# Quarter tiles of the TensorE array for the convolution and part of the products, unsplit chunk 2, blocks of 510 tokens

## Chip, cores, metric

The kernel runs on 1 core of a Trainium2 chip. The metric is the device time in microseconds (us), median of several executions. Engines: PE is TensorE (PEld its weight loads), DVE is VectorE, ACT is ScalarE, POOL is GpSimd, SP is SyncE, which here only issues DMAs.

## What is computed

`x` is 8 x 4224 tokens x 192 channels, float32. First a causal convolution of 7 taps, whose weights are a softmax for each of 8 heads (24 channels a head):

```python
w = exp(weight - max); w = w / (sum(w) + 1e-9)         # (8 heads, 7 taps)
y[b, s, h, :] = sum_k w[h, k] * xpad[b, s + k, h, :]   # causal
```

Then, with y as input:

```python
gate_pre = sum_k conv_w[k] * ypad[:, k:k+S, :]         # 5 taps for each channel, causal
gate = 1 / (1 + exp(-gate_pre))
out = (gate * (y @ w_val)) @ w_out                     # both matrices 192 x 192
```

## The kernel before

The host lays out the input; the kernel does all arithmetic. The batch is seen as 2 streams of 4 sequences each, end to end, 16936 tokens a stream with padding. A stream is cut into **supers** of mostly 976 tokens (2 runs of 488, of which 972 are new), and a super into two **blocks** of mostly 486 tokens (`SPLIT`). The 192 channels are two **chunks**: chunk 1 has 16 channels of each head (128 channels, on 128 partitions, once for each stream: parts 0 and 1, tile `xa`), chunk 2 has 8 of each head (64 channels, both streams on 128 partitions: part 2, tile `xb`).

Convolution (`mm`, line 504). A matmul takes 128 consecutive positions of 64 channels as its stationary operand (from `xin`, which `xw` fills) and the head's band matrix (`band`, 128 x 122) as its moving operand, and gives 122 outputs on 64 partitions. Two such matmuls, for the two halves of the output partitions, use the array's column halves (shape 128*64). A super takes 48 of these float32 matmuls; the trace records each as two weight loads and two matmuls. ACT copies the banks to `e` (line 521), and DMAs issued by SP move the rows to the channel order of `xa` and `xb` (line 538).

Gate. For each part ACT multiplies by the first tap (line 592), DVE adds the four others (line 598), ACT takes the sigmoid (line 604).

Products. `product` makes V = y @ w_val and O = (gate * V) @ w_out in four pieces by chunk: `p11` (128 to 128 channels, line 643, for each stream), `p21` (chunk 2 into chunk 1, line 632, on the array's row halves, 64*128), `p22` (chunk 2 to chunk 2 with a block-diagonal matrix, line 648), `p12` (chunk 1 into chunk 2, line 619, column halves, plain float32). Pieces 11, 21 and 22 run in float32r: the operand is split into a high part (ACT cast, lines 575 and 700) and the rest (POOL subtraction, lines 579 and 704), and three passes are summed:

```python
            def passes(q):
                h, l = halfs(q)
                return (wh[kind], h), (wl[kind], h), (wh[kind], l)
```

V leaves PSUM in the multiplication with the gate: on DVE for parts 1 and 2 (line 689), and for part 0 through an ACT copy `va` (line 680) and POOL (line 683). O leaves by an ACT copy to `ot` (line 716), and SP issues one store for a block.

Order. `Scheduler` simulates the engines with a cost for each operation and writes out one order for each engine; priorities are a block's due time (`tau`, spaced by `BLOCK`) plus an offset of the kind of operation (`PR`). For PE it knows modes (C for column halves, R for row halves, F for the full array), and prefers to stay in a mode. The kernel follows that order, so each engine's queue is in order. PSUM: 6 banks (`pv`) for convolution and products, 2 (`pg`) for the gate taps.

At the start PE multiplies zeros (line 391), ACT and DVE make the band, and DVE decodes the weight matrices, which come as 64-bit floats (lines 403 to 424).

Of the kernel before, what the change touches and what calls it, by code (L numbers as in the profile page):

```python
# [20 lines left out]
HALO = KG - 1  # L21
WIN, WK = 122, 128
# [5 lines left out]
MB = 488  # L28
# [4 lines left out]
RUNS = [122, 244] + [488] * 16 + [332]  # L33
SPLIT = {122: [240], 244: [484], 488: [486, 486], 332: [484, 176]}
# [3 lines left out]
def cuts(n):  # L38
    return [(o, min(WIN, n - o)) for o in range(0, n, WIN)]


class Super:
    def __init__(self, g, start):
        self.g, self.start, self.run = g, start, RUNS[g]
        self.toks = 2 * self.run
        self.blocks = SPLIT[self.run]
        assert sum(self.blocks) == self.toks - HALO
        self.runs = (self.run, self.run // 2)
        self.cuts = tuple(cuts(r) for r in self.runs)
        self.items = []  # L50
        self.banks = []
# [4 lines left out]
        self.loads = []  # L56
        self.where = {}
        for c in (1, 0):
            w = 128 * len(self.cuts[c])
            for q in range(4):  # L60
                if not self.loads or self.loads[-1] + w > 1024:
                    self.loads.append(0)
                self.where[c, q] = len(self.loads) - 1, self.loads[-1]
                self.loads[-1] += w
# [15 lines left out]
FLAT = max(p.start + p.toks for p in SUPERS) + WK  # L80
AT = [3 * sum(s[2] for s in STEPS[:n]) for n in range(N + 1)]

# [19 lines left out]
class Scheduler:  # L102
    LAG = {"PE": 260, "ACT": 200, "DVE": 200, "POOL": 200, "DMA": 100}
    SAME = {"PE": 0, "ACT": 120, "DVE": 127, "POOL": 100}
    SWITCH, STICK, HASTE = 190, 10000, 2.0
    PATIENCE = {"PE": 0, "ACT": 0, "DVE": 0}
    RATE, FLIGHT, LAND = 320.0, 900, 600
# [35 lines left out]
    def run(self):  # L143
# [11 lines left out]
        mode, dma = None, 0.0  # L155
        events = [(0.0, -1, None)]
        done, order = 0, []
        n = 0
        while events:
# [11 lines left out]
            while again:  # L171
                again = False
                for e in engines:
# [30 lines left out]
                    ns = o.ns  # L204
# [4 lines left out]
                    o.eng, o.at = e, t  # L209
                    busy[e] = t + ns  # L210
                    if o.kb:
                        dma = max(dma, t + ns + self.FLIGHT) + o.kb * 1000.0 / self.RATE
                        o.end = dma + self.LAND
                    else:
                        o.end = t + ns
# [25 lines left out]
NR, NW = 384, 448  # L241
HALVES = (slice(0, 64), slice(64, 128))

POOLS = {"x": 6, "e": 9, "x1": 3, "x2": 3, "xs": 2, "g": 3, "ps": 2, "ot": 3, "va": 2, "pv": 6, "pg": 2}
FULL_OUT = ()
POOL_GATE = (0,)
BLOCK = 9400.0
PR = {
    "load": -35000, "conv": -19500, "cstep": 1000, "row": -6000, "hx": -1500, "lx": -16000,
# [7 lines left out]
def kernel(  # L257
# [15 lines left out]
    def sb(name, shape, dt=F32):  # L273
# [3 lines left out]
        "x": [sb(f"xin{i}", [WK, 1024]) for i in range(POOLS["x"])],  # L277
# [3 lines left out]
        "xs": [  # L281
            (sb(f"xh{i}", [128, 2, MB], F32R), sb(f"xl{i}", [128, 2, MB], F32R), sb(f"yh{i}", [128, MB], F32R), sb(f"yl{i}", [128, MB], F32R))
            for i in range(POOLS["xs"])
        ],
        "g": [(sb(f"ga{i}", [128, 2, MB]), sb(f"gb{i}", [128, MB])) for i in range(POOLS["g"])],
        "ps": [
            {q: (sb(f"ph{q}{i}", [128, MB], F32R), sb(f"pl{q}{i}", [128, MB], F32R)) for q in range(3) if q not in FULL_OUT}
            for i in range(POOLS["ps"])
        ],
        "ot": [sb(f"ot{i}", [128, 3 * MB]) for i in range(POOLS["ot"])],  # L290
# [11 lines left out]

    def cast_ns(n):
# [4 lines left out]
    band = sb("band", [WK, NH, WIN])  # L308
# [11 lines left out]
    raw_v = slots["x"][-1][:, : 2 * NV].bitcast(I32)  # L320
    raw_o = slots["ot"][1][:, : 2 * NO].bitcast(I32)
    tmp = [slots["ot"][0][:, i * NV : (i + 1) * NV].bitcast(I32) for i in range(3)]
    tmp.append(slots["ot"][1][:, 2 * NO : 2 * NO + NV].bitcast(I32))
# [10 lines left out]
    boot_x, boot_ot, boot_raw = sc.buf("x"), sc.buf("ot"), sc.buf("ot")  # L334
    boot_x.slot, boot_ot.slot, boot_raw.slot = POOLS["x"] - 1, 0, 1
    sc.free["x"] = [(0, i) for i in range(POOLS["x"] - 1)]
    sc.free["ot"] = [(0, i) for i in range(2, POOLS["ot"])]
# [11 lines left out]
    for i in range(2):  # L349
        hs = slice(4 * i, 4 * i + 4)  # L350
        ld_bw.append(dma(f"bw{i}", "SP", lambda o, hs=hs: issue(o).dma_start(band[:, hs], bw[:, hs]), (), P0 + 1 + i, (), 250))
# [4 lines left out]
    t1 = sc.add("texp", "ACT", 1500, lambda o: nc.scalar.activation(warm[:, 0:1], one, AF.Exp), (z1,), P0)  # L356
# [13 lines left out]
    for i, h in enumerate((0, 4, 1, 5, 2, 6, 3, 7)):  # L370
        x = sc.add(
            f"exp{h}", "ACT", 240,
# [5 lines left out]
            f"band{h}", "DVE", 200,  # L378
# [52 lines left out]
    ld_wr = dma("wr", "SP", lambda o: issue(o).dma_start(raw_v, wr.bitcast(I32)), (), PW, (boot_x,), 404)  # L431
# [397 lines left out]
```

## Time and profile before

| | us |
|---|---|
| device time, median of 3 runs | 371.16 (369.92 to 372.65) |
| device time of the profiled execution | 370.18 |
| its span in the profile | 368.4 |
| busy in the span: PE / PEld / DVE / ACT / POOL | 356.9 / 285.2 / 340.6 / 342.6 / 289.1 |
| granted TensorE clock, mean | 0.998 |

The span runs from the first to the last instruction; 1.8 us of the device time lie outside it. Busy time is a union, so operations that overlap on their engine count once. Matmuls overlap too: the time that one costs is read from the start of one to the start of the next, not from its duration.

### The profile page before, as it was taken

Reading aid. Unit: us, or ns where it says so; the run is one execution under the profiler, and the core shown is the slowest. Engines: PE = TensorE matmul, PEld = TensorE weight load, DVE = VectorE, ACT = ScalarE, POOL = GpSimd, SP = SyncE. Lnnn points to the kernel's source line nnn. Section 1 sums busy time; section 2 is a strip of 40 time slices with the busy share of each in tenths; the row PEclk is TensorE's granted clock in tenths of the full one; section 3 lists DMA queues with packets and bytes.
Section 4 is the critical chain, followed back from the end, with each engine's and each line's share of the span. In section 5 each row is a group of like instructions: output and inputs, shape, how many; then the busy total and the mean of one; then the engine's idle time right before and its main releaser. Section 6 shows DMA issues by size and latency. Waiting matters only on the chain.

```text
span 368.4 us, 9449 instructions
## 1 busy us (share of the span) xinstructions
PE 356.9 (97%) x3362; PEld 285.2 (77%) x3362; DVE 340.6 (92%) x550; ACT 342.6 (93%) x662; POOL 289.1 (78%) x236
## 2 busy tenths in 40 slices
PE   8588999999999999999999999999999999999996
PEld 4476787787977787878888787888887878887674
DVE  4999999989999999899999999899989898999993
ACT  6459999998999999999999999999999999999985
POOL 1946998976868895969787878879696969787994
PEclk9999999999999999999999999999999999999999
DMA  7798855739495466758593939395857767444324
GB/s 244 227 322 269 263 230 210 245 129 316 161 322 228 171 221 209 283 209 285 203 294 110 328 142 322 145 315 180 290 195 233 252 225 234 163 165 162 115 81 191
DMA packets 36222, 81.87 MB, mean 222 GB/s; under 512 B 6096, under 2 KB 24400, under 8 KB 36176
## 3 DMA queue, kind: packets, MB, share of 16 engines
q1 hardware_dynamic: 35712, 80.59, 63.7%
q0 software_dynamic: 464, 0.69, 0.6%
q8 instruction: 26, 0.43, 0.5%
q14 instruction: 20, 0.16, 0.1%
HBM read 29.11 MB, written 26.01 MB: 150 GB/s over the span
## 4 chain that ended last, share of the span: by engine, by line
PE 92%; DMA 4%; ACT 1%; SPq 1%; DVE 0%; issue 0%; POOL 0%; ACTq 0%; POOLq 0%
PE bank L643 27%; PE bank L504 21%; PE bank L619 16%; PE bank L632 14%; PE bank L648 13%; DMA xb<-e 4%; PE bank L391 2%; SPq L538 1%; ACT bank L592 0%; ACT yh L575 0%; DVE bank L598 0%; DVE wlO L460 0%; POOL zero L354 0%; ACT gb L604 0%; ACT va L680 0%
## 5 line engine op out<-in xcount | busy, mean ns | idle before, releaser
L598 DVE SCALAR_TENSOR_TENSOR bank<-xa,cwt,bank 128x486 f32<-128x486 f32 (+3 forms) x216 | 151.5, 708 | 11.5 <-ACT bank L592 7.5
L504 PE MATMUL bank<-band,xin 128*64 128x122 f32 (+2 forms) x1696 | 92.6, 267 | 5.1 <-DMA xin<-xw 5.1
L504 PEld LDWEIGHTS bank<-band,xin 128*64 128x64 f32 x1696 | 89.2, 137 | 9.4 <-ACT bank L592 2.5
L704 POOL TENSOR_TENSOR pl<-ga,ph 128x486 fp32r<-128x486 f32 (+3 forms) x72 | 85.8, 1205 | 8.0 <-ACT ph L700 6.4
L579 POOL TENSOR_TENSOR xl<-xa,xh 128x972 fp32r<-128x972 f32 (+3 forms) x36 | 73.8, 2051 | 20.5 <-ACT xh L575 20.5
L598 DVE SCALAR_TENSOR_TENSOR bank<-xb,cwt,bank 128x486 f32<-128x486 f32 (+3 forms) x108 | 76.2, 706 | 1.3 <-ACT bank L592 0.5
L716 ACT COPY ot<-bank 128x486 f32<-128x486 f32 (+3 forms) x108 | 58.2, 559 | 8.8 <-PE bank L648 3.9
L521 ACT COPY e<-bank 128x488 f32<-128x488 f32 (+2 forms) x107 | 55.9, 577 | 6.0 <-PE bank L504 6.0
L683 POOL TENSOR_TENSOR ga<-va,ga 128x486 f32<-128x486 f32 (+3 forms) x36 | 43.2, 1201 | 18.4 <-ACT va L680 17.9
L579 POOL TENSOR_TENSOR yl<-xb,yh 128x486 fp32r<-128x486 f32 (+3 forms) x36 | 40.7, 1131 | 18.3 <-ACT yh L575 18.3
L598 DVE SCALAR_TENSOR_TENSOR ga<-xa,cwt,bank 128x486 f32<-128x486 f32 (+3 forms) x72 | 50.4, 701 | 2.0
L592 ACT ACTIVATE bank<-xa,cwt 128x486 f32<-128x486 f32 (+3 forms) x72 | 48.5, 673 | 0.1
L704 POOL TENSOR_TENSOR pl<-gb,ph 128x486 fp32r<-128x486 f32 (+3 forms) x36 | 43.3, 1202 | 2.0 <-ACT ph L700 2.0
L604 ACT ACTIVATE ga<-ga 128x486 f32<-128x486 f32 (+3 forms) x72 | 44.4, 618 | 0.2
L700 ACT CAST ph<-ga 128x486 fp32r<-128x486 f32 (+3 forms) x72 | 42.4, 602 | 0.0
L619 PE MATMUL bank<-ga,wfO 128*64 128x242 f32 (+3 forms) x288 | 36.1, 370 | 0.0
L575 ACT CAST xh<-xa 128x972 fp32r<-128x972 f32 (+3 forms) x36 | 35.7, 991 | 0.5 <-DMA xa<-e 0.5
L619 PE MATMUL bank<-xa,wfV 128*64 128x242 f32 (+3 forms) x288 | 34.4, 362 | 0.7 <-DMA xa<-e 0.7
L643 PE MATMUL bank<-xh,whV 128*128 128x486 f32 (+3 forms) x72 | 28.7, 399 | 1.2 <-DVE gb L689 1.2
L643 PE MATMUL bank<-ph,whO 128*128 128x486 f32 (+3 forms) x72 | 29.5, 409 | 0.0
L619 PEld LDWEIGHTS bank<-ga,wfO 128*64 128x64 f32 x288 | 18.2, 136 | 11.7 <-issue 6.8
L643 PE MATMUL bank<-pl,whO 128*128 128x486 f32 (+3 forms) x72 | 27.2, 378 | 0.0
(87 smaller groups left out, 660.7 us busy)
## 6 DMA issues: line engine op xcount, KB each, us to landing
xin<-xw SPq DMA_DIRECT2D x51, 512.0 KB, 6.3
out<-ot SPq DMA_DIRECT2D x32, 729.0 KB, 4.5
xa<-e SPq DMA_DIRECT2D x64, 244.0 KB, 2.4
xb<-e SPq DMA_DIRECT2D x128, 61.0 KB, 2.1
out<-ot SPq DMA_DIRECT2D x2, 726.0 KB, 3.5
xin<-xw SPq DMA_DIRECT2D x2, 384.0 KB, 7.4
xa<-e SPq DMA_DIRECT2D x4, 166.0 KB, 2.2
band<-bw SPq DMA_DIRECT2D x2, 244.0 KB, 3.0
```

What stands on the lines that cost most here:

```text
L504: nc.tensor.matmul(at(pc)[P, j * run + a : j * run + a + n], lhsT=t[:, off + 128 * w + 64 * h : off + 128 * w + 64 * h + 64], rhs=band[:, ...
L521: nc.scalar.copy(at(eb)[:, :n], at(pc)[:, :n])
L579: nc.gpsimd.tensor_tensor(out=s[2 * c + 1], in0=views(n)[c], in1=s[2 * c].bitcast(F32), op=ALU.subtract)
L592: lambda o, n=n, i=i, pg=pg, m=m: nc.scalar.mul(at(pg)[:, :m], part(n, i, 0), cwt[:, i // 2, 0:1]),
L598: v.scalar_tensor_tensor(out=acc if k < KG - 1 else gate(i), in0=part(n, i, k), scalar=cwt[:, i // 2, k : k + 1], in1=acc, op0=ALU.mult, o ...
L604: sig[i] = sc.add(f"s{n}.{i}", "ACT", 0.823 * m + 110, lambda o, i=i, gate=gate: nc.scalar.activation(gate(i), gate(i), AF.Sigmoid), (d, t ...
L619: nc.tensor.matmul(a[P, c], lhsT=wf[kind][:, W12 : W12 + 64], rhs=full_x(q)[:, c], start=new and i == 0, stop=not new and i == 1,)
L632: nc.tensor.matmul(at(acc[q])[:, :m], lhsT=a[P, W21 : W21 + 128], rhs=b[P], start=new[q] and i == 0, stop=not new[q] and i == 2,)
L643: nc.tensor.matmul(at(acc[q])[:, :m], lhsT=a[:, W11 : W11 + 128], rhs=b, start=new and i == 0, stop=not new and i == 2)
L648: nc.tensor.matmul(at(acc[2])[:, :m], lhsT=a[:, W22 : W22 + 128], rhs=b, start=new and i == 0, stop=not new and i == 2)
L704: nc.gpsimd.tensor_tensor(out=l, in0=gate(q), in1=h.bitcast(F32), op=ALU.subtract)
L716: lambda o, q=q, ob=ob, po=po, m=m: nc.scalar.copy(at(ob)[:, q * m : (q + 1) * m], at(po[q])[:, :m]),
```

## The change

- Convolution: windows of 64 positions give up to 58 outputs. A matmul uses a quarter of the array (64 rows, 64 columns); four of them, two heads' groups on the two row halves by two output halves, go one after another to the four quarters, and the row halves write two PSUM banks. A super of 1024 tokens (1020 new) has 9 cuts of 57 and 5 of 52 tokens, each for two pairs of groups: 112 matmuls.
- Piece 21 of V and O: four quarter matmuls in plain float32 (`mm21`). Piece 22 of V: column halves in plain float32 (`mmcol`). Piece 22 of O: quarters in plain float32, for two blocks at once; O's chunk 2 for two blocks lies in two banks (`x`, `y`), one for each stream, and is stored for the pair.
- Chunk 2 is no longer split: its ACT casts and POOL subtractions go, for y and for the gated values.
- Part 2 is gated on POOL like part 0 (one more ACT copy, DVE only has part 1).
- Blocks have 510 tokens; the last super has two blocks of 450 (before 484 and 176). Loads of `xin` have up to 640 columns (before 1024), 6 a super (before 3). Buffers, priorities and the planner's constants change with it, and the planner's mode R becomes Q (quarters), to which the convolution belongs as well. At the start, row moves of the first two supers are issued by POOL with ACT or SP, and the loads of three supers come first.

```diff
-WIN, WK = 122, 128
+WIN, WK = 58, 64
-MB = 488
+MB = 512
-RUNS = [122, 244] + [488] * 16 + [332]
-SPLIT = {122: [240], 244: [484], 488: [486, 486], 332: [484, 176]}
+RUNS = [116, 256] + [512] * 15 + [452]
+SPLIT = {116: [228], 256: [508], 512: [510, 510], 452: [450, 450]}
+LOADW = 640
...
 def cuts(n):
-    return [(o, min(WIN, n - o)) for o in range(0, n, WIN)]
+    k = -(-n // WIN)
+    s = -(-n // k)
+    return [(o, min(s, n - o)) for o in range(0, n, s)]
...
+        self.sets = []
         for c in (1, 0):
-            per = MB // self.runs[c]
-            for a in range(0, 4, per):
-                self.banks.append((c, list(range(a, min(4, a + per)))))
...
+            per = max(1, MB // self.runs[c])
+            for a in range(0, 2, per):
+                self.sets.append((c, [2 * i for i in range(a, min(2, a + per))]))
...
-POOL_GATE = (0,)
+POOL_GATE = ((0, 2),)
...
-            def mm(o, c=c, qs=qs, pc=pc, run=run, cc=cc, src=src, xb=xb):
...
-                    i, off = src[j]
-                    t = at(xb[i])
                     for w, (a, n) in enumerate(cc):
+                        i, off = p.where[c, q, w]
+                        t = at(xb[i])
                         for h, P in enumerate(HALVES):
-                            nc.tensor.matmul(
-                                at(pc)[P, j * run + a : j * run + a + n],
-                                lhsT=t[:, off + 128 * w + 64 * h : off + 128 * w + 64 * h + 64],
-                                rhs=band[:, head(c, q, h), :n], start=True, stop=True,
-                            )
-
-            ns = sum(2 * (0.80 * n + 8.5) for _, n in cc) * len(qs)
+                            for r, K in enumerate(HALVES):
+                                nc.tensor.matmul(
+                                    at(pcs[r])[P, j * run + a : j * run + a + n],
+                                    lhsT=t[K, off + 64 * h : off + 64 * h + 64],
+                                    rhs=band[K, head(c, q + r, h), :n], start=True, stop=True,
+                                )
+            ns = sum(2 * max(0.80 * n + 10, CONV_MIN) for _, n in cc) * len(qs)
...
+    def mm21(kind, banks, rhs, m):
+        def emit(o):
+            new = [b.open(0, 1) for b in banks]
+            for h, P in enumerate(HALVES):
+                for b, K, x in zip(banks, HALVES, new):
+                    nc.tensor.matmul(
+                        at(b.buf)[P, :m], lhsT=wf[kind][K, W21 + 64 * h : W21 + 64 * h + 64], rhs=rhs()[K], start=x, stop=not x,
+                    )
+        return emit
...
+    def mmcol(kind, off, pieces, m):
+        def emit(o):
+            new = [b.open(h) for b, h, _, _ in pieces]
+            for (b, h, w, rhs), x in zip(pieces, new):
+                nc.tensor.matmul(at(b.buf)[HALVES[h], :m], lhsT=wf[kind][:, off + w : off + w + 64], rhs=rhs(), start=x, stop=not x)
+        return emit
...
+            w = m * len(V_SPLIT)
+            h = sc.add(f"hx{n}", "ACT", cast_ns(w), hx, L[0], t0 + PR["hx"], None, (xb[0], xsb))
+            hs = [h, sc.add(f"lx{n}", "POOL", 2.0 * w + 265, lx, [h] + L[0], t0 + PR["lx"], None, (xb[0], xsb))]
...
+        o21 = sc.add(f"V21.{n}", "PE", fp32(m), mm21("V", (a, b), lambda: part(2), m), L[1] + fv, t0 + PR["V21"], "Q", (a.buf, b.buf, xb[2]))
...
+            sc.add(f"V12.{n}", "PE", fp32(m), mmcol("V", W12, [(c, h, 0, lambda h=h: part(h)) for h in range(2)], m), L[0] + fv, t0 + PR["V12"], "C", (c.buf, xb[0])),
+            sc.add(f"V22.{n}", "PE", fp32(m), mmcol("V", W22, [(c, h, 64 * h, lambda: part(2)) for h in range(2)], m), L[1] + fv + [zw[0]], t0 + PR["V22"], "C", (c.buf, xb[2])),
...
-            if q in POOL_GATE:
+            pb = pv[q].buf
+            if q in POOL_GATE[n % len(POOL_GATE)]:
...
+            if q in O_SPLIT:
+                sb_ = psb[q] = sc.buf("ps")
+                h = sc.add(f"hg{n}.{q}", "ACT", cast_ns(m), lambda o, q=q, sb_=sb_: nc.scalar.copy(at(sb_)[0][:, :m], gate(q)), (d,), t0 + PR["cast"], None, (gb[q], sb_))
...
+            x, y = Bank(), Bank()
+            def mm22(o):
+                new = [b.open(0, 1) for b in (x, y)]
+                for h, P in enumerate(HALVES):
+                    for b, K, w in zip((x, y), HALVES, new):
+                        nc.tensor.matmul(
+                            at(b.buf)[P, :m], lhsT=wf["O"][K, W22 + K.start : W22 + K.start + 64], rhs=gates[h](2)[K], start=w, stop=not w,
+                        )
+            o22 = sc.add(f"O22.{pair[0]}", "PE", fp32(m), mm22, [d[2] for d in dfs] + fo, t0 + PR["O22"], "Q", [x.buf, y.buf] + [b[2] for b in gbs])
+            pieces = [(b, h, 0, lambda h=h, q=q: gates[h](q)) for q, b in enumerate((x, y)) for h in range(2)]
+            o12 = sc.add(
+                f"O12.{pair[0]}", "PE", 2 * fp32(m), mmcol("O", W12, pieces, m), [d[q] for d in dfs for q in range(2)] + fo,
+                t0 + PR["O12"], "C", [x.buf, y.buf] + [b[q] for b in gbs for q in range(2)],
             )
...
+            send([(x, [o12, o22]), (y, [o12, o22])], k, tau[pair[1]], f"{pair[0]}p")
```

## Rows read from the trace of the kernel before

**Rows 1.** The page's first part: busy us of each engine, share of the span.

```profile
PE 356.9 (97%) x3362; PEld 285.2 (77%) x3362; DVE 340.6 (92%) x550; ACT 342.6 (93%) x662; POOL 289.1 (78%) x236
```

**Rows 2.** The page's fourth part: the chain that ended last, by engine and line.

```profile
PE 92%; DMA 4%; ACT 1%; SPq 1%; DVE 0%; issue 0%; POOL 0%; ACTq 0%; POOLq 0%
PE bank L643 27%; PE bank L504 21%; PE bank L619 16%; PE bank L632 14%; PE bank L648 13%; DMA xb<-e 4%; PE bank L391 2%; SPq L538 1%; ACT bank L592 0%; ACT yh L575 0%; DVE bank L598 0%; DVE wlO L460 0%; POOL zero L354 0%; ACT gb L604 0%; ACT va L680 0%
```

**Rows 3.** Windows: length; busy PE, PEld, DVE, ACT, POOL; clock, DMA share, GB/s.

```profile
7.60:30.00 22.40, 15.68 (x243) 13.66 (x242) 20.64 (x45) 12.31 (x27) 12.98 (x17) 1.00 0.79 263
...
132.67:152.36 19.69, 19.69 (x194) 16.00 (x193) 19.22 (x30) 19.22 (x38) 14.74 (x13) 1.00 0.70 237
152.36:172.04 19.68, 19.68 (x190) 16.14 (x188) 18.48 (x29) 19.07 (x37) 16.02 (x13) 1.00 0.69 236
...
350.00:368.40 18.40, 15.21 (x108) 11.16 (x106) 12.07 (x26) 12.91 (x32) 13.00 (x14) 0.96 0.35 136
```

**Rows 4.** Timeline of PE over one super, 152.36 to 172.04: start, us, operation.

```profile
152.36 5.17 PE L504 MATMUL bank<-band,xin 128*64 128x122 f32 x96
157.36 0.99 PE L619 MATMUL bank<-ga,wfO 128*64 128x242 f32 x8
158.18 0.99 PE L619 MATMUL bank<-xa,wfV 128*64 128x242 f32 x8
159.10 0.49 PE L643 MATMUL bank<-ph,whO 128*128 128x486 f32 x1
159.44 0.38 PE L643 MATMUL bank<-ph,wlO 128*128 128x486 f32 x1
159.66 0.39 PE L643 MATMUL bank<-pl,whO 128*128 128x486 f32 x1
...
166.46 0.45 PE L632 MATMUL bank<-pl,whO 64*128 64x486 f32 x2
166.84 0.49 PE L643 MATMUL bank<-xh,whV 128*128 128x486 f32 x1
167.17 0.38 PE L643 MATMUL bank<-xh,wlV 128*128 128x486 f32 x1
```

**Rows 5.** Timeline of PE around 8.1 us: convolution matmuls of 61 columns.

```profile
7.90 0.46 PE L504 MATMUL bank<-band,xin 128*64 128x61 f32 x10
```

**Rows 6.** Timeline of the weight loads in the same stretch.

```profile
7.91 0.38 PEld L504 LDWEIGHTS bank<-band,xin 128*64 128x64 f32 x10
```

**Rows 7.** Timeline of the weight loads around 144.6 us, row halves.

```profile
144.58 0.19 PEld L632 LDWEIGHTS bank<-pl,whO 64*128 64x128 f32 x2
```

**Rows 8.** Groups by shape, whole span: count, busy us, mean ns of one.

```profile
L504 PE MATMUL bank<-band,xin 128*64 128x61 f32 x16 | 0.7, 226 | 0.0
...
L598 DVE SCALAR_TENSOR_TENSOR bank<-xa,cwt,bank 128x240 f32<-128x240 f32 x6 | 2.8, 460 | 0.0
...
L521 ACT COPY e<-bank 128x332 f32<-128x332 f32 x6 | 2.3, 455 | 0.0
```

**Rows 9.** Groups by shape of ACT, window 152.36 to 172.04.

```profile
L521 ACT COPY e<-bank 128x488 f32<-128x488 f32 x6 | 3.1, 588 | 0.0
...
L575 ACT CAST yh<-xb 128x486 fp32r<-128x486 f32 x2 | 1.3, 632 | 0.0
...
L700 ACT CAST ph<-gb 128x486 fp32r<-128x486 f32 x2 | 1.2, 595 | 0.0
L680 ACT COPY va<-bank 128x486 f32<-128x486 f32 x2 | 1.2, 588 | 0.0
```

**Rows 10.** Groups by shape of DVE, same window.

```profile
L598 DVE SCALAR_TENSOR_TENSOR bank<-xa,cwt,bank 128x486 f32<-128x486 f32 x12 | 8.6, 726 | 1.0 <-ACT bank L592 0.7
...
L689 DVE TENSOR_TENSOR gb<-bank,gb 128x486 f32<-128x486 f32 x2 | 1.3, 665 | 0.1
```

**Rows 11.** Groups by shape of POOL, same window.

```profile
L579 POOL TENSOR_TENSOR yl<-xb,yh 128x486 fp32r<-128x486 f32 x3 | 3.5, 1171 | 1.0 <-ACT yh L575 1.0
...
L683 POOL TENSOR_TENSOR ga<-va,ga 128x486 f32<-128x486 f32 x2 | 2.5, 1233 | 1.2 <-ACT va L680 1.2
```

More of the change, by code (lines that the diff above doesn't have):

```diff
@@ L79 @@
 TM = max(p.toks for p in SUPERS)
-FLAT = max(p.start + p.toks for p in SUPERS) + WK
+FLAT = max(p.start + p.toks for p in SUPERS) + 2 * WK
 AT = [3 * sum(s[2] for s in STEPS[:n]) for n in range(N + 1)]
+PAIRS = []
+for _n in range(N):
+    if PAIRS and len(PAIRS[-1]) == 1 and STEPS[_n][0] == STEPS[_n - 1][0] and STEPS[_n][2] == STEPS[_n - 1][2]:
+        PAIRS[-1] += (_n,)
+    else:
+        PAIRS.append((_n,))
 def head(c, q, half):
@@ L276 @@
     slots = {
[L277 removed]
+        "x": [sb(f"xin{i}", [128, LOADW]) for i in range(POOLS["x"])],
         "e": [sb(f"e{i}", [128, MB]) for i in range(POOLS["e"])],
@@ L301, in small, with either, leave @@
         return 0.72 * n + 105
+    def either(n):
+        return {"ACT": 0.72 * n + 105, "DVE": 1.042 * n + 70}
+    def leave(o, dst, src):
+        if o.eng == "ACT":
+            nc.scalar.copy(dst, src)
+        else:
+            v.tensor_copy(dst, src)
     def cast_ns(n):
         return 0.823 * n + 100
-    band = sb("band", [WK, NH, WIN])
+    band = sb("band", [128, NH, WIN])
     hwt = sb("hwt", [128, NH, KW])
@@ L552, in part, with fp32, thrice, __init__ @@
         return x1[:, i] if i < 2 else x2
-    for n, (g, off, m) in enumerate(STEPS):
+    def fp32(m):
+        return 2 * (0.83 * m + 10)
+    def thrice(m):
+        return 3 * (0.431 * m + 9.5)
+    class Bank:
+        def __init__(self):
+            self.buf, self.fresh, self.made = sc.buf("pv"), [True, True], []
+        def open(self, *halves):
+            new = any(self.fresh[h] for h in halves)
+            for h in halves:
+                self.fresh[h] = False
+            return new
@@ new lines, in mm21, with mm11 @@
+    def mm21(kind, banks, rhs, m):
[7 more added lines that the diff above has]
+        return emit
+    def mm11(kind, bank, rhs, split, m, mode):
+        def emit(o):
+            new = bank.open(0, 1)
+            d = at(bank.buf)[:, :m]
+            if split is not None:
+                h, l = split()
+                for i, (a, b) in enumerate(((wh[kind], h), (wl[kind], h), (wh[kind], l))):
+                    nc.tensor.matmul(d, lhsT=a, rhs=b, start=new and i == 0, stop=not new and i == 2)
+            elif mode == "F":
+                nc.tensor.matmul(d, lhsT=wf[kind][:, W11 : W11 + 128], rhs=rhs(), start=new, stop=not new)
+            else:
+                for h, P in enumerate(HALVES):
+                    nc.tensor.matmul(d[P], lhsT=wf[kind][:, W11 + 64 * h : W11 + 64 * h + 64], rhs=rhs(), start=new, stop=not new)
+        return emit
@@ L702, in lg @@
-            def lg(o, q=q, gsplit=gsplit, gate=gate):
-                h, l = gsplit(q)
-                nc.gpsimd.tensor_tensor(out=l, in0=gate(q), in1=h.bitcast(F32), op=ALU.subtract)
-            l = sc.add(f"lg{n}.{q}", "POOL", 2.0 * m + 265, lg, (h, d), t0 + PR["rest"], None, (gb, psb))
-            dh[q], dl[q] = [h], [l]
-        keep = {0: [gb, psb], 1: [gb, psb], 2: [psb, gb]}
-        ro = product("O", po, lambda q, gsplit=gsplit: gsplit(q), lambda q, gate=gate: gate(q), dh, dl, df, tuple(t0 + PR["O" + k] for k in "FRC"), f32=FULL_OUT, keep=keep)
@@ L730 @@
+    for pair in PAIRS:
+        for n in pair:
+            gate_and_value(n)
+        output(pair)
     order = sc.run()
@@ L784, in packed @@
         return p.reshape(128, -1)
-    bw = np.full((WK, NH, WIN), FILL, f)
+    bw = np.full((128, NH, WIN), FILL, f)
     for k in range(KW):
         j = np.arange(WIN)
-        bw[j + k, :, j] = weight[:, k]
+        for r in (0, WK):
+            bw[r + j + k, :, j] = weight[:, k]
     arrays = {
```

437 lines of the change are left out of this document (226 added, 211 removed), and 7 rows, old and new, of the table PR.

## Prediction

> **What bounds the kernel now.** I read the busy times first [rows 1]: PE 97%, ACT 93%, DVE 92%. Shares so close don't name a limit, so I went to the chain that ended last [rows 2]: 92% of it is PE, with five matmul lines as its parts and 4% of DMA. The windows show where [rows 3]: from the middle on, a super (972 new tokens) takes 19.69 us, and PE is busy in all of it (19.68 of 19.68), at the full granted clock, with ACT at 19.07 and DVE at 18.48. The two other engines have 0.6 and 1.2 us of air in a super. So what the change is worth is PE time in a super, until ACT takes over. 16936 tokens at 19.69 us for 972 make 343.1 us; the other 25.3 us of the 368.4 are the start and the end (in the stretch from 7.6 to 30 us PE is busy for 15.68 of 22.40, in the last one for 15.21 of 18.40) and small blocks. I carry that sum over and price the super.
>
> **PE, item by item, for a super of 1020 tokens.** Costs are distances from start to start.
>
> Float32 passes of column halves: eight records of 242 or 244 columns take 158.18 - 157.36 = 0.82 us [rows 4], that is four steps of a pair, 0.205 us for 243 columns, or 0.843 ns a column. A float32 matmul pair over 510 columns (two records each) thus costs 2 x 0.430 = 0.86 us. V12, V22 and O12 of two blocks are six such: 5.16 us.
>
> Float32r passes of the full array: 159.66 - 159.44 = 0.22 us for 486 columns [rows 4], by column 0.230 for 510. Piece 11 of V and O is 2 x 2 x 2 x 3 = 24 passes: 5.52 us.
>
> Quarters, pieces 21 and 22 of O: V21 and O21 for each block and one O22 for the pair, five in all. No row has a quarter matmul. If the four quarters run side by side, as the two column halves do now, each item costs what a pair of halves does, 0.86 us: 4.30. If the row halves took turns it would be 8.60. I take the first: the two weight loads of a row-halves pair lie together within 0.19 us [rows 7], the length of one. Per token these items are no gain for piece 21 (0.86 for 510 tokens against three passes of 0.22 for 486); O22 gains (0.43 a block against 0.66), V22 loses as much as 21.
>
> Convolution: now 5.00 us a super (157.36 - 152.36) for 96 records, a pair every 0.104 us [rows 4]. After: 112 matmuls, or 28 groups of four, two records each, 56 steps. How long is a step with 52 to 57 columns? By columns it would be 0.104 x 57/122 = 0.049 us. The nearest row are the ten matmuls of 61 columns, five pairs of column halves, in the first super: 0.46 us from the first start to the last end [rows 5], of which one lasts 0.226 [rows 8], so four steps take some 0.234, 58 ns each. The loads of the same stretch, ten in 0.38 us with 0.137 for one, give 60 [rows 6]. Columns alone would ask for 52, so here the weight loads of 64 columns set the step, and they will with 57 and 52 columns too. I take 58.5 ns: 56 x 0.0585 = 3.28 us. The lower end is the column rate, 2.64; the upper one is all eight records of a step in a row at the rate of those rows (ten matmuls and ten loads in 0.24 us, 12 ns each): 96 ns a step, 5.4 us.
>
> Mode changes: 0.34 instead of 0.22 for the first full pass [rows 4], and about 0.09 before it; from row halves back to the full array 0.38 and 0.33 instead of 0.22 each. About 0.2 us a change, four in a super now. There are three modes after; with three to six changes I take 0.87.
>
> The sum is 5.16 + 5.52 + 4.30 + 3.28 + 0.87 = **19.13 us for 1020 tokens**, 18.75 ns a token against 20.26 now. The gain is the convolution's: it falls from 5.14 to 3.21 ns a token, and the products' higher price eats about a quarter of it.
>
> **The other engines in that super.** ACT loses the casts of part 2 (1.3 and 1.2 us busy) and gains two copies `va` (1.2) [rows 9]. Wider blocks cost (588 - 455)/(488 - 332) = 0.85 ns a column [rows 8, 9]; 24 columns over 34 single and two double instructions are 0.78 us. So 19.07 - 1.3 + 0.8 = 18.6 of 19.13: the air shrinks from 0.6 to 0.5 us. DVE loses two gate multiplications (0.665 each) and pays (726 - 460)/246 = 1.08 ns a column on 26 instructions [rows 8, 10]: 18.48 - 1.33 + 0.67 = 17.8. POOL loses two subtractions of y (1.17 each) and two of the gated values (taken like the gate's, 1.23), and gains two gates (1.233) [rows 11]; with wider blocks about 14.3 us of 19.13. The new wait is the gate of part 2: it stands in ACT's queue behind casts and in POOL's behind subtractions (2 to 3 us at the worst), and V's bank and the pair's O wait for it. PE has a second block's work meanwhile, so I cost it at nothing; without that cover it is the 1.23 us of a POOL gate a block.
>
> The Trainium skill weighs in here: TensorEngine Tiling (Array Packing), section PSUM Bottleneck, says that tiling speeds up TensorE but not the evacuation of PSUM, which may become the limit. The trace agrees that ACT, which does most of that work, is 0.6 us from the limit.
>
> DMA: a load moves 64 positions for at most 57 outputs, so a super reads 3584 x 512 B = 1.84 MB for 1020 tokens, before 1.57 MB for 972. The rest scales with tokens (81.87 MB in all, 4.70 a super). At 19.13 us that is 268 GB/s, beside 236 at a DMA share of 0.69 [rows 3], so a share of about 0.79. SP issues 21 DMAs a super (6 loads, 12 row moves, 3 stores) instead of 17; at about half a microsecond each that fills half of its time. Hidden.
>
> **Total.** 16936/1020 x 19.13 = 317.6 us. The start and end I carry over (25.3) and add 1.0: the last block has 450 instead of 176 tokens, and in the final chain of gate, cast, subtraction, matmul and copy each step is 0.85 ns (ACT) to about 2.5 ns (POOL, 1233/486) a column longer, some 1.4 us, less a little for band tiles of half the width. Span 343.9; with the 1.8 us outside it 345.7. The profiled execution was 1.0 us below the median (370.18 against 371.16), so I name **347 us** as the median, 6.5% less. The same with 18.7 to 19.5 us for a super is 339 to 353.
>
> **Rivals.**
> (a) ACT becomes the bound. It has 0.5 us of air and gets more work that empties PSUM. If stalls of the in-order queue keep it at 5.5% idle instead of 3%, a super takes 18.6/0.945 = 19.7 us and the time is 327.1 + 26.3 + 2.8 = **356**. For it: ACT at 97% already. Against it: at 97% it did not stop PE once in a super [rows 3].
> (b) The other side: instructions can't be handed to four quarters fast enough. A step has eight records; at the 12 ns each of [rows 5, 6] it takes 96 ns, the convolution 5.4 us and a super 21.3, so 353.7 + 26.3 + 2.8 = **383**, slower. It decides from 86 ns a step: 20.26 x 1.020 = 20.66 us is break-even, minus 15.85 for all but the convolution leaves 4.81 for 56 steps. Against it: in those rows the load of a tile sets the pace, so 12 ns is what was asked for, not what can be had; a pair of row-halves loads lies within the time of one [rows 7]. For it: no row shows a denser stream that lasts.
> The Trainium skill speaks for (b): TensorE: Matmul & The Clock Gate, section "Wait — 56ns, not 53.3ns?", says that matmuls never start less than about 25 ns apart. Four a step would then be 100 ns, a convolution of 5.6 us and a time of 386. As a mean, the pairs of 61 columns, two starts in 58 ns, neither break that rule nor need it.
> (c) The quarters don't run side by side: row halves take turns in all quarter work. Convolution 6.55, pieces 21 and 22 8.6, a super of 26.7 us, **472**. Against it: row halves run together today, and only float32 in them is new.
> (d) Loads overlap better with four tiles: the convolution at the column rate, 2.64 us. PE would need 18.5 and ACT 18.6, so a super of 18.6: 308.8 + 29.1 = **338**.
>
> **How the numbers follow.** Forecast 0.60, (a) 0.20, (b) 0.12, (c) 0.03, (d) 0.05. The range reaches from (d) to past (a), 338 to 360; (b), (c) and a worse start, some 0.18, lie outside. A change below 1% can't be told from none here (three runs spread over 0.7%). Faster by over 1%: forecast, (a) and (d), 0.84 with a little taken off for a bad start; slower: (b) and (c) with the worst of (a), 0.14; 0.02 between.
>
> **What would show it.** A super's period near 19.1 us with PE busy throughout; convolution bursts of 3.3 us for 224 records and steps of 58 ns; quarter items at 0.86 us; ACT at 18.6 us a super. Wrong if the burst is 5 us or longer (b), if quarter items cost 1.7 (c), if PE idles before ACT's copies or POOL's gates (a), or if the start, where DVE is busy for 20.64 of 22.40 us [rows 3], is longer by more than 3 us: the 26.3 us of start and end are the least founded term.

## The result, and the profile after

The changed kernel takes 354.82 us (median of 4 runs, 353.77 to 356.29) against 371.47 of the kernel before (4 runs beside it): a ratio of 0.956 (95% interval 0.950 to 0.961), 4.4% less. The forecast was 347, 6.5% less, with a range of 338 to 360. The profiled execution took 356.29 us, its span is 354.5. About a third of the expected gain is missing. The execution that the profile shows is 1.5 us above the median.

The page of the changed kernel, busy time of each engine and the chain that ended last, to set beside [rows 1, 2]:

```profile
PE 338.6 (96%) x5232; PEld 190.6 (54%) x5232; DVE 315.5 (89%) x494; ACT 316.6 (89%) x589; POOL 247.3 (70%) x189
...
PE 50%; ACT 20%; DMA 12%; DVE 9%; issue 3%; POOL 3%; SPq 2%; ACTq 0%; DVEq 0%
```

The first line alone would say "PE-bound as before". The second doesn't: PE was 92% of the chain, now it is half; ACT, DMA and DVE hold 41%. Windows of the changed kernel (columns as in [rows 3]): the start, nine supers, one settled super, three settled supers, the end:

```profile
7.60:30.00 22.40, 17.12 (x452) 11.74 (x451) 16.25 (x45) 10.49 (x24) 9.98 (x15) 0.77 0.65 224
70.78:251.35 180.57, 177.43 (x2812) 100.08 (x2808) 166.28 (x243) 170.49 (x311) 129.92 (x92) 1.00 0.73 254
240.49:259.48 18.99, 18.99 (x315) 10.96 (x313) 17.99 (x27) 18.69 (x35) 14.38 (x10) 1.00 0.78 265
251.35:308.33 56.98, 56.98 (x940) 32.86 (x936) 53.91 (x79) 56.10 (x103) 43.19 (x31) 1.00 0.73 252
330.00:354.50 24.50, 19.80 (x116) 9.47 (x112) 15.41 (x26) 15.03 (x30) 15.37 (x13) 0.94 0.31 121
```

A settled super is the forecast's: 18.99 us, PE busy throughout. But only the last part of the run is settled. The nine supers from 70.78 to 251.35 us take 180.57 us, 9.7 more than nine of 18.99; ACT is busy in 94.4% of that stretch (170.49 of 180.57) and in 98.5% of the settled one (56.10 of 56.98). The settled super on PE (start, us, operation), to set beside [rows 4]:

```profile
240.49 1.27 PE L542 MATMUL bank<-band,xin 64*64 64x57 f32 x72
241.58 1.04 PE L809 MATMUL bank<-g,wfO 64*64 64x510 f32 x8
242.44 1.03 PE L616 MATMUL bank<-g,wfO 64*64 64x510 f32 x8
243.30 1.22 PE L542 MATMUL bank<-band,xin 64*64 64x57 f32 x72
244.34 1.04 PE L616 MATMUL bank<-xb,wfV 64*64 64x510 f32 x8
245.31 0.49 PE L629 MATMUL bank<-xh,whV 128*128 128x510 f32 x1
245.65 0.39 PE L629 MATMUL bank<-xh,wlV 128*128 128x510 f32 x1
...
255.96 1.88 PE L644 MATMUL bank<-g,wfO 128*64 128x510 f32 x8
257.67 1.02 PE L644 MATMUL bank<-xb,wfV 128*64 128x510 f32 x4
```

Read start to start: a convolution burst of 72 records is 1.04 us (244.34 - 243.30), 18 steps of 57.8 ns; a quarter item 0.86 (242.44 - 241.58); two column items 1.71 (257.67 - 255.96); the first full pass 0.34.

What ACT waits for in the nine supers, us in total, times, longest; and the longest of the kernel before over nine of its supers (77.26 to 254.94 us), where no cast waits for rows:

```profile
ACT xh L677 <- DMA xa<-e: 7.7, 6, 2.5
ACT bank L694 <- DVE g L700: 1.3, 4, 0.5
```

```profile
ACT ot L716 <- PE bank L632: 2.1, 7, 0.3
```

One such wait on ACT, SP and DVE (start, us, operation, idle time before it):

```profile
172.51 1.05 ACT L677 CAST xh<-xa 128x1020 fp32r<-128x1020 f32 x1 [1.29 <-DMA xa<-e]
...
168.04 1.25 SPq L575 DMA_DIRECT2D xa<-e  x2
169.38 3.16 SPq L525 DMA_DIRECT2D xin<-xw  x6
...
174.18 0.76 DVE L700 SCALAR_TENSOR_TENSOR bank<-xb,cwt,bank 128x510 f32<-128x510 f32 x1 [1.01 <-ACT bank L694]
```

SP issues the row moves of `xa` at 168.04 and six loads right behind them; the cast that needs the rows runs at 172.51, with ACT idle for 1.29 us, and DVE, which stands behind ACT, for 1.01. A row move's median from issue to landing is 3.2 us for `xa` and 3.1 for `xb` (before 2.4 and 2.1). PE then waits for ACT's copies. That shows only in part as idle time, 3.1 us in the nine supers (180.57 - 177.43), because the last matmul is still running during a short wait:

```profile
142.17 1.21 PE L616 MATMUL bank<-g,wfO 64*64 64x510 f32 x8
143.41 0.32 PE L542 MATMUL bank<-band,xin 64*64 64x57 f32 x2
143.88 1.21 PE L542 MATMUL bank<-band,xin 64*64 64x57 f32 x67 [0.16 <-ACT ot L335]
```

From 142.17 to 143.88 PE gets one quarter item and two records of a burst done in 1.71 us; the item alone takes 0.86 in the settled super, and only 0.16 us is idle time.

The same happens at the start, while loads fill the DMA engines (share 1.01 from 7.6 to 14 us): four copies of ACT stand behind a DMA.

```profile
10.38 3.85 ACTq L575 DMA_DIRECT2D xb<-e  x4
15.19 1.35 ACTq L575 DMA_DIRECT2D xa<-e  x2
16.58 1.63 ACT L335 COPY e<-bank 128x256 f32<-128x256 f32 x4 [8.04 <-DMA xb<-e]
...
18.42 1.04 PE L616 MATMUL bank<-xb,wfV 64*64 64x228 f32 x8 [1.68 <-DMA xb<-e]
```

The first product starts at 18.42 us (before at 14.17).

### The profile page after: what moved, and what is told of

The parts are those of the page before. It is cut to its first block, busy times and chain, and to the rows that moved or that the text cites. A ratio compares the mean times of both kernels' runs of the same rounds, so it can differ in the third digit from the quotient of the medians.

```text
span 354.5 us, 12997 instructions
## 1 busy us (share of the span) xinstructions
PE 338.6 (96%) x5232; PEld 190.6 (54%) x5232; DVE 315.5 (89%) x494; ACT 316.6 (89%) x589; POOL 247.3 (70%) x189
## 4 chain that ended last, share of the span: by engine, by line
PE 50%; ACT 20%; DMA 12%; DVE 9%; issue 3%; POOL 3%; SPq 2%; ACTq 0%; DVEq 0%
PE bank L629 17%; PE bank L644 13%; PE bank L616 10%; PE bank L542 8%; DVE bank L700 5%; DMA xin<-xw 5%; DMA xa<-e 5%; ACT e L335 4%; ACT bank L694 4%; ACT g L706 3%; ACT ot L335 3%; ACT va L734 2%; ACT xh L677 2%; ACT ph L749 2%; PE bank L809 2%
## 5 line engine op out<-in xcount | busy, mean ns | idle before, releaser
L700 DVE SCALAR_TENSOR_TENSOR bank<-xa,cwt,bank 128x510 f32<-128x510 f32 (+3 forms) x204 | 146.5, 737 | 8.0 <-ACT bank L694 5.1
L737 POOL TENSOR_TENSOR g<-va,g 128x510 f32<-128x510 f32 (+3 forms) x68 | 85.8, 1264 | 46.7 <-ACT va L734 32.1
L753 POOL TENSOR_TENSOR pl<-g,ph 128x510 fp32r<-128x510 f32 (+3 forms) x68 | 84.3, 1254 | 22.5 <-ACT ph L749 22.4
L681 POOL TENSOR_TENSOR xl<-xa,xh 128x1020 fp32r<-128x1020 f32 (+3 forms) x34 | 73.0, 2147 | 18.5 <-ACT xh L677 17.4
L700 DVE SCALAR_TENSOR_TENSOR bank<-xb,cwt,bank 128x510 f32<-128x510 f32 (+3 forms) x102 | 75.2, 737 | 9.2 <-ACT bank L694 6.7
L542 PEld LDWEIGHTS bank<-band,xin 64*64 64x64 f32 x3728 | 64.5, 137 | 33.8 <-issue 12.1
L542 PE MATMUL bank<-band,xin 64*64 64x57 f32 (+7 forms) x3728 | 67.4, 222 | 4.4 <-issue 2.2
L706 ACT ACTIVATE g<-g 128x510 f32<-128x510 f32 (+3 forms) x102 | 65.6, 650 | 1.3 <-DVE g L700 1.3
L335 ACT COPY e<-bank 128x512 f32<-128x512 f32 (+3 forms) x101 | 56.3, 606 | 11.7 <-DMA xb<-e 8.0
L335 ACT COPY ot<-bank 128x510 f32<-128x510 f32 (+3 forms) x99 | 56.3, 605 | 5.8 <-PE bank L809 2.7
```

The costliest lines, as they stand in the source:

```text
L335: nc.scalar.copy(dst, src)
L542: nc.tensor.matmul(at(pcs[r])[P, j * run + a : j * run + a + n], lhsT=t[K, off + 64 * h : off + 64 * h + 64], rhs=band[K, head(c, q + r, h ...
L681: nc.gpsimd.tensor_tensor(out=l, in0=view(0)[:, cols], in1=h.bitcast(F32), op=ALU.subtract)
L700: v.scalar_tensor_tensor(out=acc if k < KG - 1 else gate(i), in0=part(i, k), scalar=cwt[:, i // 2, k : k + 1], in1=acc, op0=ALU.mult, op1= ...
L706: sig[i] = sc.add(f"s{n}.{i}", "ACT", 0.823 * m + 110, lambda o, i=i: nc.scalar.activation(gate(i), gate(i), AF.Sigmoid), (d, t2), tp + PR ...
L737: lambda o, q=q, vb=vb: nc.gpsimd.tensor_tensor(out=gate(q), in0=at(vb)[:, :m], in1=gate(q), op=ALU.mult),
```

## Experiments

The theory: rows that land late meet an ACT with too little air to take the wait up, in the nine supers and, at the start, behind the loads of three supers. The rivals: the convolution's steps or the quarters' hand-out cost more than they seem; ACT loses time because it issues DMAs itself; it is the written order alone.

**Each half of the change alone, in the old priorities.** `conv_only` takes the convolution and its loads, `products_only` all but these. Both keep the blocks of 486 tokens, so the wider blocks are in neither.

```diff
 # conv_only, against the kernel before; mm as in the change
-WIN, WK = 122, 128
+WIN, WK = 58, 64
+LOADW = 640
 # products_only, against the changed kernel; mm as before
-WIN, WK = 58, 64
+WIN, WK = 122, 128
```

> The kernel before with the quarter-tile convolution alone (its products, splits, gates and blocks of 486 tokens stay). PE's price for a super of 972 tokens falls from 19.69 us to about 18.1 (convolution 3.4 instead of 5.0), while ACT keeps its 19.07. Theory that ACT is next: a super takes 19.2 to 19.5 us, PE shows idle time before ACT's copies, 363 to 368 us, 1 to 2% below the kernel before. Rival, PE's gain passes through: supers of 18.1 to 18.4 us, 343 to 350 us.

> The changed kernel with the convolution of the kernel before (128 positions, column halves, 122 outputs) and its blocks of 486 tokens; unsplit chunk 2, quarters for pieces 21, pairs for O22 and two gates on POOL stay. By the prices, PE needs 5.0 for the convolution, 4.9 for column halves, 5.3 for full passes, 4.1 for quarters and 0.8 for mode changes, 20.1 us for 972 tokens against 19.69: 375 to 381 us, 1 to 3% slower than the kernel before, with ACT idle for a tenth. Rival, the relief of ACT is itself worth something: 365 us or less.

Measured: 391.53 us (ratio 1.053, 1.048 to 1.058) and 393.67 (1.060, 1.057 to 1.063). Both expectations missed, and nothing follows for the parts: the priorities of another mix of work give an order in which engines stand. Beside the next pair they show the size of that effect, some 20 us.

**The same with priorities searched anew**, for a planner that also knows that an issue waits for the DMA eight before it on its queue and that rows land later (`LAND` 1300 instead of 600 ns). In the trace of the changed kernel the DMAs of SP and ACT take eight completion semaphores in turn, and none is issued before the last one on its semaphore has landed (the closest 16 ns after it):

```diff
+                        ring = self.rings.setdefault(e == "POOL", [])
+                        ns += max(0.0, ring[-self.RING] - t) if len(ring) >= self.RING else 0.0
```

> The kernel before with the quarter convolution and the 640-column loads alone (products, blocks of 486 tokens and chunk 2's split as before), and with priorities searched for these costs, so that the order fits the work. PE's sum for a super of 972 tokens falls from 19.69 us by the difference of the two convolutions, 5.00 - 3.28, to 17.97; ACT keeps its 19.07 us. Theory: ACT becomes the bound, a settled super takes 19.1 to 19.4 us and the time is 361 to 366 us, some 2 % less. Rival (PE alone sets the time, ACT's work is always covered): a super near 18.1 us and 343 to 347 us. A time above 371 us would mean that the convolution's later rows cost more than its speed gives.

> The changed products alone (quarters for pieces 21 and 22 of O, column halves for 22 of V, chunk 2 not split, pairs of blocks) with the convolution, loads and blocks of 486 of the kernel before, and with priorities searched for these costs. PE's sum for a super of 972 tokens: convolution 5.00, six column pieces 4.92, full passes 24 x 0.22 = 5.28, five quarter items 4.10, mode changes 0.87, together 20.2 us against 19.69; ACT some 18.3. Theory: PE-bound, a settled super of 20.0 to 20.4 us and 374 to 383 us, 1 to 3 % slower. Rival (the products are themselves a gain, because ACT has air again): a super of 19.6 us or less and 371 us or less.

Measured: the convolution alone 370.82 us (ratio 0.999, 0.996 to 1.001), the products alone 375.74 (1.012, 1.008 to 1.016). Page and windows of the convolution alone:

```profile
PE 352.8 (96%) x5602; PEld 260.2 (71%) x5602; DVE 336.5 (91%) x552; ACT 340.4 (92%) x663; POOL 290.1 (79%) x237
...
7.60:30.00 22.40, 17.99 (x469) 15.44 (x469) 17.36 (x45) 10.89 (x26) 13.23 (x19) 0.62 0.79 249
42.93:142.40 99.47, 96.58 (x1585) 69.95 (x1580) 94.14 (x145) 96.21 (x183) 81.09 (x62) 1.00 0.71 244
142.40:203.03 60.63, 59.70 (x980) 44.39 (x973) 57.26 (x89) 59.82 (x114) 51.94 (x39) 1.00 0.72 256
203.03:297.16 94.13, 93.90 (x1591) 70.73 (x1587) 90.81 (x140) 93.31 (x179) 77.75 (x59) 1.00 0.74 251
```

and of the products alone:

```profile
PE 363.6 (97%) x3288; PEld 225.5 (60%) x3288; DVE 319.3 (85%) x516; ACT 324.7 (87%) x624; POOL 250.1 (67%) x200
...
7.60:30.00 22.40, 17.50 (x227) 12.09 (x228) 18.20 (x43) 10.94 (x25) 11.24 (x16) 1.00 0.72 250
160.13:259.91 99.78, 99.78 (x925) 62.50 (x923) 83.20 (x126) 90.34 (x171) 69.41 (x51) 1.00 0.63 231
```

With the convolution alone ACT is the bound: busy in 98.9% of 142 to 297 us. The eight supers there take 19.34 us each on average (154.76 in all), as expected, against 19.69 [rows 3]; the time missed the expected 361 to 366 us. These 0.35 us would make 6 us over 17.4 supers, but the kernel's time is ACT's work and the time in which ACT has none: 340.4 + 27.8 us, before 342.6 + 25.8 [rows 1]. The rest of the run does not gain: the five or so supers from 42.93 to 142.40 us take 19.9 each, and up to 30 us, where the granted clock is 0.62, before 1.00 [rows 3], ACT gets 10.89 us of work done instead of 12.31. The products alone are PE-bound, as expected: five supers of 19.96 us, all of it PE. But they take ACT's work down to 324.7 us. So neither part makes the kernel faster, and the whole change does: the convolution frees PE, and the products free ACT. The whole change takes ACT's work down to 316.6 us. The two parts add up to less: 342.6 less 17.9 (products) and 2.2 (convolution) leaves 322.5. The other 6 us are left for the wider blocks (ACT has 589 instructions, with the products alone 624), which no run tests by themselves.

**What sets the convolution's step.** Half the moving columns, then also half the stationary ones (the output's slice is cut to match, and the banks are set to zero once at the start; both left out here):

```diff
-                                    lhsT=t[K, off + 64 * h : off + 64 * h + 64],
-                                    rhs=band[K, head(c, q + r, h), :n], start=True, stop=True,
+                                    lhsT=t[K, off + 64 * h : off + 64 * h + 32],
+                                    rhs=band[K, head(c, q + r, h), : n // 2], start=True, stop=True,
```

> The changed kernel; each convolution matmul computes only the first half of its columns (28 or 26 instead of 57 or 52; half of the convolution's outputs are left out). A step of four quarters takes 60 ns in the changed kernel. If weight loads of 64 columns or the hand-out of eight records set it, it stays at 55 to 61 ns; if columns set it, it falls to about 30.

> As the run with half the columns, and each weight load has 32 instead of 64 columns (three quarters of the convolution's outputs are left out). If weight loads set the step, it falls to 30 to 40 ns; if the hand-out of eight records does, it stays at 55 to 61.

PE's timeline with half the columns, then with half of both:

```profile
242.31 1.20 PE L542 MATMUL bank<-band,xin 64*64 64x28 f32 x72
243.33 0.64 PE L616 MATMUL bank<-xb,wfV 64*64 64x510 f32 x4
```

```profile
240.51 0.82 PE L542 MATMUL bank<-band,xin 64*32 64x28 f32 x72
241.25 0.70 PE L616 MATMUL bank<-xb,wfV 64*64 64x510 f32 x4
```

18 steps take 1.02 us (57 ns each) and 0.74 (41 ns). Fewer moving columns change nothing, narrower weights do: the weight load of 64 columns sets the step, as the forecast read from [rows 5, 6]. The device times, 355.76 and 351.96 us, of one run each, say little more.

**Who issues, how many loads, how many bytes.** `rows_sp` lets SP issue what ACT issued at the start; `big_loads` has loads of 1280 columns in 7 buffers instead of 640 in 14; `half_store` stores half of each output's columns.

```diff
-    ISSUE = {"SP": nc.sync, "POOL": nc.gpsimd, "ACT": nc.scalar}
+    ISSUE = {"SP": nc.sync, "POOL": nc.gpsimd, "ACT": nc.sync}
...
-LOADW = 640
+LOADW = 1280
...
-at(ob)[:, k * m : e * m]
+at(ob)[:, k * m : k * m + (e - k) * m // 2]
```

> The changed kernel, with the first super's row moves that ACT issued given to SP; the planned order is the same. Theory: at the start ACT's queue stands on these six DMAs, the copies of the second super's banks come late, PE waits and its clock halves; without them the products of the first block start 2 to 4 us earlier than at 18.4 us, the granted clock stays at full, and the time is 350 to 353 us. Rival: the start waits for loads and row landings whoever issues them, and the time stays within 1 us of 354.8.

> The changed kernel with loads of up to 1280 columns, 3 a super instead of 6, in half as many buffers; the order of everything else is the same to the instruction. The trace of the changed kernel has eight completion semaphores that the DMAs of SP and ACT take in turn, so a DMA is not issued before the one eight places ahead has landed; with 6 loads in a row, row moves stand behind loads that take 6 to 8 us. Theory: with 3 loads the row moves leave earlier, ACT's cast xh waits less for them, the supers between 70 and 212 us take 19.0 to 19.6 us instead of 20.3, the start is shorter too, and the time is 344 to 349 us. Rival, it is the bytes on the DMA engines: these are the same, a load of twice the size lands later, and the time is 354 to 358 us.

> The changed kernel; each store to memory moves only the first half of its columns, so half of the output is left out (13 MB of 84.6 MB). Order and engine work are the same. Theory that the supers of 20 to 21 us between 70 and 212 us are long because row moves land late beside loads and stores: with less traffic they fall to 19.0 to 19.5 us and the time to 346 to 350 us. Rival, ACT is so full that any disorder of the queues stays, whatever the DMAs do: 353 to 356 us.

Measured: `rows_sp` 354.06 us (ratio 0.953, 0.950 to 0.957), `big_loads` 353.7 (0.952, 0.947 to 0.958): neither differs measurably from the changed kernel, and both theories missed. `rows_sp` does not show that ACT's own issues cost nothing: SP issues loads until 11.6 us and the row moves of `xb` only from 12.18 on, and the first product starts at 20.74 us instead of 18.42. It shows that SP is no better place for them. With half as many loads ACT still waits for `xa` for 6.2 us in the nine supers. `half_store` takes 349.83 (0.943, 0.939 to 0.946), 5 us less, a time as expected; nine supers in its trace, from the same point of the order on:

```profile
70.59:247.41 176.82, 175.05 (x2812) 99.85 (x2808) 166.01 (x243) 170.33 (x311) 129.80 (x92) 1.00 0.65 220
```

The same ACT work (170.33 us) in 3.8 us less time, and the three ACT waits for `xa` that are left come to 4.1 us instead of 7.9 over the whole run. The time shows that the traffic of the stores costs (the four runs of each kernel do not overlap). That it costs by delaying these rows is less certain, because the loss in the nine supers also differs between traces with all the stores. In `rows_sp` ACT waits for `xa` for 4.5 us in them, and they take

```profile
72.92:250.41 177.49, 175.96 (x2812) 99.53 (x2808) 166.36 (x243) 170.55 (x311) 129.78 (x92) 1.00 0.75 259
```

that is 0.7 us more than with half the stores and 3.1 less than in the changed kernel; in `big_loads` they take 178.94.

**Air for ACT.** Sigmoids on half of their columns, in an unchanged order.

```diff
-nc.scalar.activation(gate(i), gate(i), AF.Sigmoid)
+nc.scalar.activation(gate(i)[:, : m // 2], gate(i)[:, : m // 2], AF.Sigmoid)
```

> The changed kernel in the same order of every engine, with each sigmoid on half of its columns (half of the gate stays without sigmoid); this frees some 1.3 us of ACT in a super of 18.99. Theory (ACT is too full to absorb rows that land late, so the supers between 70 and 232 us take 20.3 instead of 19.0): they fall to 19.0 to 19.4 us and the time to 346 to 349 us. Rival (the rows' landing itself, or the order of PE, holds the supers, whatever air ACT has): 353 to 356 us, and the casts' waits for row moves stay in PE's gaps.

Measured: 350.61 us (ratio 0.945, 0.940 to 0.950). Windows of the nine supers, and ACT's wait in them:

```profile
70.25:246.75 176.50, 174.78 (x2813) 98.13 (x2809) 165.47 (x242) 160.78 (x311) 129.72 (x91) 1.00 0.76 260
...
ACT xh L677 <- DMA xa<-e: 7.3, 6, 3.3
```

Between the two expectations. ACT waits as long for the rows as before (7.3 us, changed kernel 7.7), but the nine supers take 4.1 us less, and three of them run at the settled rate (18.99 to 19.00), in the changed kernel one. The time, 4.2 us less, with runs that do not overlap, shows that air on ACT helps; 5.6 of the 9.7 us are lost with air as well. How much a full ACT costs these supers is not settled: in `rows_sp`, where ACT has all its work, they take only 1.0 us more than here.

**An order that expects late rows.** `after_fit` is the changed kernel with the planner of the second pair, priorities searched anew; `big_fit` adds the loads of 1280 columns.

> The changed kernel with another order: its planner is told of the eight semaphores and of later landing, and its priorities are searched again; the work is the same. Theory that the missing 8 us are row moves that land later than the planned order supposes: an order that knows it loses less, 345 to 350 us. Rival, ACT is too full for any order: 353 to 357 us.

> The changed kernel with loads of 1280 columns in 7 buffers (3 a super instead of 6) and an order whose planner knows that an issue waits for the DMA eight before it on its queue and that rows land later, with priorities searched again. Theory (the loss against the settled supers is one of rows that come late through that queue, and half as many loads shorten it): supers of 19.0 to 19.2 us from 70 us on, a start 2 to 4 us shorter, 346 to 351 us. Rival (the order alone did it in the kernel with 640 columns): 351.5 to 353.5 us, as there.

Measured: `after_fit` 352.46 us (ratio 0.947, 0.944 to 0.951), the best full version, some 0.7% below the changed kernel with intervals that just touch. `big_fit` 360.45 (0.972, 0.966 to 0.978). Windows of nine supers of `after_fit`, and ACT's longest sum of waits in them:

```profile
74.91:246.89 171.98, 171.81 (x2806) 99.26 (x2802) 164.13 (x238) 168.78 (x308) 128.56 (x90) 1.00 0.76 263
246.89:285.26 38.37, 38.37 (x628) 22.37 (x624) 36.06 (x53) 37.37 (x69) 28.66 (x21) 1.00 0.75 265
...
ACT ot L341 <- PE bank L635: 1.9, 5, 0.5
ACT bank L700 <- DVE g L706: 1.1, 2, 0.6
```

In `after_fit` no cast waits for rows in these supers, and they take 171.98 / 9 = 19.11 us each. But the super before them takes 21.96 us (52.95 to 74.91) instead of 18.49 (52.29 to 70.78), so the fair cut has ten supers. First `after_fit`, then the changed kernel:

```profile
52.95:246.89 193.94, 192.48 (x3117) 110.59 (x3116) 185.24 (x269) 189.40 (x346) 145.46 (x102) 1.00 0.77 268
```

```profile
52.29:251.35 199.06, 195.83 (x3116) 110.37 (x3112) 183.97 (x269) 188.98 (x345) 145.57 (x102) 1.00 0.74 256
```

So the same operations take 5.1 us less there in another order, with 0.8 us of casts' waits for rows instead of 7.7: most of the loss is not in the operations but in when things come. Only part shows in the time, 2.4 us by the medians, where 345 to 350 us were expected: this order's settled super is 19.18 us (38.37 / 2) instead of 18.99. `big_fit` missed: its settled super is 19.14 us, as expected, but its order leaves gaps on PE between 51.74 and 102.90 us, told at the end.

## Why the prediction was right in range and short in gain

**The super: right.** 19.13 us forecast, 18.99 measured, term by term in the timeline above: convolution 3.39 us in its three bursts (forecast 3.28, at 57.8 ns a step where 58.5 was taken), five quarter items 4.45 (4.30), 24 full passes 5.87 (5.52), six column items 5.28 (5.16); the five mode changes lie in these figures, and the clean items leave 0.9 us for them (forecast 0.87). So are ACT at 18.69 (18.6), DVE 17.99 (17.8), POOL 14.38 (14.3), DMA 265 GB/s at a share of 0.78 (268, 0.79).

**The range: by luck.** The forecast's own span of 18.7 to 19.5 us for a super gave 339 to 353 us, and 354.82 lies outside it. It lies in 338 to 360 only because that range was drawn past rival (a), whose 356 is nearer than 347. One of the signs of being wrong that it names came, a start longer by more than 3 us: the first product is 4.2 us later.

**The gates of part 2 on POOL: right.** In the nine supers PE waits for a POOL gate once; two blocks' work covers the rest.

**Rivals (b), (c), (d): refuted.** Quarters run side by side: an item costs 0.86 us, not 1.7. The hand-out isn't the limit either: with narrow weights four matmuls and four loads go in 41 ns. The Trainium skill's rule that spoke for (b) (TensorE: Matmul & The Clock Gate, section "Wait — 56ns, not 53.3ns?": never less than about 25 ns between starts) would make that step an estimated 100 ns; the trace does not agree for quarters. Nor did the trace of the kernel before for column halves: in the burst of [rows 4] the two records of the first pair start within 0.01 us, which the forecast's mean, two starts in 58 ns, hides. And (d) needed the column rate, but the columns don't matter.

**"Hidden", said of the DMAs: the step that failed.** The forecast had the traffic right and took it for covered, because it counted queue time and bandwidth, not how long a row move takes to land among the loads. Measured, the median move of `xa` lands 3.2 us after its issue instead of 2.4, and ACT waits 7.7 us for such rows in the nine supers. Little was left to hide it: ACT is busy for 18.7 of 19 us. The air that the forecast itself put at 0.5 us a super is less than one wait (1.29 us above, 2.5 at the longest).

**"The start and end I carry over (25.3) and add 1.0": mis-sized by that.** Measured by the same sum, 354.5 - 16.604 x 18.99 = 39.2 us instead of 26.3. 9.7 of it are the nine supers, in which the rate isn't yet the settled one, which is no start at all; the other 3.2 are the start and end proper, where the first product comes 4.2 us later, its rows on their way while the loads of three supers land, and where the granted clock is lower (last section). Up to 1.5 of the 12.9 us may belong to the profiled execution, which is that much above the median. Half of rival (a) thus came true: it priced an ACT idle for 5.5%, and in the nine supers it is idle for 5.6%. But what ACT waits for is the rows, not the banks that it empties, and it passes.

**"The gain is the convolution's ... and the products' higher price eats about a quarter of it": right for PE, wrong for the kernel.** The convolution alone gave 0.999, the products alone 1.012, the whole change, with its wider blocks, 0.956. The Trainium skill's warning (TensorEngine Tiling (Array Packing), section PSUM Bottleneck), that tiling speeds up TensorE but not the evacuation of PSUM, agrees with the convolution alone, where ACT at 98.9% is the limit; but ACT's casts and sigmoids fill it too, and the products help because they drop casts.

**Open.** Which part of the late rows is DMA traffic and which is the queue's order is not separated: half the stores gave 5 us, half as many loads nothing that can be measured, the new order 2.4 us in the end. Nor is it settled why the nine supers take from 177.49 to 180.57 us in traces with the same work in them, or what the wider blocks are worth. The slower start (and its lower clock) was not removed by any run.

## What to carry to other kernels

Multiply a settled stage's price by the whole length only after asking when it is settled: where a second engine has less air in a stage than one late transfer costs, late transfers show in the time. Look at what a change frees on every engine that is near its limit; two changes that gain nothing alone can gain together, when each frees what the other needs (here with wider blocks beside them, which were not tried alone). A part tried alone in an order searched for something else measures the order.

## What the hardware showed that I had not expected

At the start the granted clock is lower with the quarter convolution: 0.77 and 0.62 from 7.6 to 30 us in the changed kernel and with the convolution alone, 1.00 in the kernel before [rows 3] and with the products alone. In the changed kernel it falls at 13.83 us and is back at 24.07:

```profile
7.60:13.83 6.23, 4.03 (x214) 3.56 (x214) 5.95 (x19) 0.26 (x1) 3.28 (x6) 1.00 1.01 387
13.83:24.07 10.24, 7.16 (x135) 5.31 (x135) 5.32 (x13) 5.28 (x13) 4.28 (x7) 0.50 0.57 173
```

When it falls PE has been idle since 13.0 us, and it stays so until 15.23. In the kernel before PE is busy for 4.38 and 6.35 us of the same two stretches, and the clock stays at 1.00; what makes the difference is not shown. PE's busy time up to 30 us is longer in the changed kernel (17.12 us against 15.68), but that is not more work: at the lower clock a matmul lasts longer. The burst of 72 records at 21.11 us takes 2.11 us, in the settled super 1.04.

After a gap it can fall later too, once an order leaves one. PE in `big_fit`:

```profile
61.86 1.10 PE L650 MATMUL bank<-xb,wfV 128*64 128x510 f32 x4 [2.18 <-DVE g L749]
62.77 3.58 PE L650 MATMUL bank<-g,wfO 128*64 128x510 f32 x8
66.27 1.08 PE L622 MATMUL bank<-g,wfO 64*64 64x510 f32 x8
```

After 2.18 us of waiting the eight records from 62.77 on take 3.50 us, where eight such take 1.71 in the settled super: the granted clock of that stretch is 0.51, the lower of the two levels, 1.2 GHz. There a gap cost its length and some 1.8 us more. A second such stretch lies from 83.26 to 86.68 us. But the clock is the smaller part of what this order loses: the two supers from 51.74 to 102.90 us take 51.2 us, 12.9 more than at its settled rate. PE's idle time is 5.3 us of that, and the two stretches at the lower clock are some 3.4 at most (half of 6.8).
